# A decode kernel of four attention layers: the last four K tiles of each layer moved ahead of the last four V tiles, with four buffers for p

## The chip, the cores and the metric

The kernel runs on one core of a Trainium2 chip. The metric is the device time in microseconds (us), the median of several runs. Intervals are 95% intervals.

PE is the matmul engine, DVE the vector engine, ACT the scalar engine, SP the engine whose queue issues the large transfers (SPq in the profiles), DMA the 16 transfer engines. PEld is PE loading its weights, POOL the general-purpose engine, which does next to nothing here. The granted clock is the share of full speed at which PE was allowed to run. L541 in a profile is line 541 of that run's kernel. K28 is the K tile of a layer's head 28 in order of work, softmax 31 the softmax of its last head.

## The reference

One token goes through four layers, A, B, A, B. Each is attention over a cache of 8192 positions with 32 heads of 192, plus a residual:

```python
q = (layernorm(x) @ wq).reshape(32, 192)
scores = einsum("hd,hkd->hk", q, k_cache) * 192 ** -0.5      # k_cache: 32 x 8192 x 192, bf16
o = einsum("hk,hkd->hd", softmax(scores), v_cache)
x = x + o.reshape(1, 32 * 192) @ wo                          # x: 640
```

Every head brings a K tile and a V tile of 3.1 MB each, used once per layer. A and B are read twice, by layers 0 and 2 and by layers 1 and 3.

## The kernel before

The program is built from two lists. `steps` is the order of the work: `m` multiplies a K tile by q on DVE while PE sums the products, `s` is the softmax of one head, `v` the product with V on PE, `wc` and `wo` the turning and projecting of finished heads. `plan` is the order of the transfers. Tiles go into eight slots; a transfer is issued when the slot's previous tile is worked off.

```python
NSLOT = 8
KEPT = {0: {("k", 0), ("v", 0)}, 1: {("v", 28), ("v", 29), ("v", 30), ("v", 31)}}
...
            for p in range(H):
                if p > 0 and p % HEADS_W == 0:                 # p = 10, 20, 30
                    b = p // HEADS_W - 1
                    steps.append(("wc", l, b))
                    if p <= H - HEADS_W:
                        plan.append(("wo", l, b))
                        steps.append(("wo", l, b))
                if first_load("k", l, p) == ("k", l, p):
                    plan.append(("k", l, p))
                ...
                elif p < H - 2:
                    part = [("m", l, p), ("s", l, p), ("v", l, p)]
                elif p == H - 2:
                    part = [("m", l, p)]
                else:
                    part = [("s", l, p - 1), ("m", l, p), ("v", l, p - 1), ("s", l, p), ("v", l, p)]
                steps += part
                plan += [n for n in part if n[0] == "v" and first_load(*n) == n]
            ...
            plan.append(("wo", l, 2))
            steps.append(("wo", l, 2))
```

The program of every engine is written in the order of `steps`, so a V product that stands behind softmax 31 there does not start before PE's part of that softmax in the timelines below. The four V tiles of `KEPT[1]` stay in their slots from layer 1 to layer 3, so layer 2 has only four slots that turn over.

How one head's softmax and V product stand on the engines (cut):

```python
            def softmax(h):
                ev_s = DV.op(... tensor_reduce(s_sb[par][:], S[:] ...), ev_S[h], ...)      # waits for PE's sums
                ev_m = DV.op(... tensor_reduce(m_bf[par][:], s_sb[par][:], AX.X, ALU.max), ev_s, ...)
                e = PE.op(... matmul(QM[...], lhsT=m_bf ...), ev_m, ...)
                ev_n = DV.op(... tensor_reduce(negm[par][:], QM[...], AX.X, ALU.max, negate=True), e, ...)
                ev_p[h] = AC.op(... activation(p_sb[par][:], s_sb[par][:], ACT.Exp ...), ev_n, ...)
                e = PE.op(... matmul(TB[...], ... rhs=l_col ...), ev_p[h], ...)
                ev_rl[h] = ... DV.op(... reciprocal(rl[par][:], TB[...]), e, ...)          # the last step of a softmax

            def values(h):
                PE.wait(need(nv_), ev_p[h], last["O"][par])
                for m in range(J // 2):
                    e = PE.op(... matmul(OB[par][...], lhsT=p_sb[par][:, j:j + 2], rhs=t[...]) ...)
                ...                                        # ACT copies OB to o_sb, scaled; PE gathers o_sb later
```

## Time and profile before

| | before |
|---|---|
| median, us | 2004.94 of three runs, 2004.62 once a fourth was added |
| span of the profiled run | 2000.9 us |
| read from memory | 848.36 MB |
| rate where it is steady | 428 to 431 GB/s |

The page's slices (40 equal parts of the span; DMA is the busy share of the transfer engines in tenths, GB/s what they moved):

```profile
DMA  9999999999999999999999999999999999999997
GB/s 410 430 430 431 429 429 430 431 431 428 426 431 431 428 430 431 430 430 430 429 380 431 429 428 431 431 428 429 431 428 421 429 430 430 430 428 430 430 430 307
...
HBM read 848.36 MB, written 0.00 MB: 424 GB/s over the span
```

The rate is flat, so the kernel is bound by its transfers. The Trainium skill, "DMA: Bandwidth & Descriptors", Specifications, gives 435 GB/s as the ceiling of the fabric, and the 430 here agree with it. 848.36 MB at 430 GB/s are 1973 us; only the remaining 28 us of the span can be gained by reordering. The slices that fall well short are the first, the one of 380 in the middle and the last.

The windows around the middle one, the passage from layer 1 to layer 2. Columns: the stretch in us, its length, busy time (instructions) of PE, PEld, DVE, ACT and POOL, granted clock of PE, share of DMA, GB/s:

```profile
core 0: us, PE busy (x) PEld busy (x) DVE busy (x) ACT busy (x) POOL busy (x), PEclk, DMA share, GB/s
1004.00:1012.00 8.00, 7.03 (x54) 0.76 (x33) 4.58 (x6) 1.08 (x4) 0.00 (x0) 0.88 0.92 391
1012.00:1020.00 8.00, 6.23 (x149) 5.66 (x150) 0.17 (x1) 1.35 (x5) 0.00 (x0) 0.97 0.76 316
1020.00:1028.00 8.00, 5.82 (x96) 4.28 (x93) 3.58 (x12) 0.73 (x2) 0.54 (x1) 0.50 0.85 332
```

Here the rate drops to 316 GB/s: layer 2's wq comes in parts, and slots for them come free only as layer 1 ends. The end of layer 2, same columns:

```profile
1495.00:1500.00 5.00, 1.88 (x7) 0.50 (x4) 3.67 (x5) 0.44 (x2) 0.00 (x0) 0.75 1.00 428
1500.00:1505.00 5.00, 5.00 (x15) 0.00 (x0) 3.65 (x3) 0.00 (x0) 0.00 (x0) 0.57 0.99 422
1505.00:1510.00 5.00, 3.74 (x44) 1.05 (x35) 1.33 (x4) 1.15 (x4) 0.00 (x0) 1.00 0.90 367
```

One mild dip, to 367. And the end of the program, from the timeline (start, duration, engine, line, operation, tiles; in brackets what ended an idle time):

```profile
1984.53 1.47 PE L541 MATMUL O<-pool,p_sb 128*2 128x384 bf16 x32
...
1987.67 0.17 DVE L530 RECIPROCAL small<-TB 128x1 f32<-128x1 f32 x1 [1.18 <-PE TB L526]
...
1988.68 2.48 PE L541 MATMUL O<-pool,p_sb 128*2 128x384 bf16 x32
...
1991.21 0.94 ACT L556 ACTIVATE o_sb<-O,small 128x192 f32<-128x192 f32 x2 [2.25 <-PE O L541]
...
1992.21 1.44 PE L580 MATMUL TB<-small,o_sb 128*64 128x1 f32 x12 [1.04 <-ACT o_sb L556]
...
1993.58 2.56 PE L462 MATMUL YB<-oT,pool 128*128 128x1 bf16 x60
...
1997.38 0.16 DVE L628 TENSOR_TENSOR x_bf<-small,YB 128x5 bf16<-128x5 f32 x1 [9.54 <-PE YB L462]
```

Read it from L530 on, the end of softmax 31. Of the V work only V31 (32 matmuls, L541, at 1988.68) follows; V30 (at 1984.53) was already done inside the softmax. Then come the copy (L556), the gather (L580) and the projection (L462), and the result is there at 1997.4, 9.5 us after softmax 31.

### The profile page before, as it was taken

To read this page: it belongs to the slowest core of one execution; us is meant where nothing else is said; L and a number is where in the kernel's file an instruction comes from. 1 tells how busy PE (TensorE), PEld (TensorE's weight loads), DVE (VectorE), ACT (ScalarE), POOL (GpSimd) and SP (SyncE) were. 2 spreads that over 40 slices of the span, in tenths; PEclk is the share of its full clock that TensorE was granted. 3 is DMA by queue.
4 is the path that set the end of the run, shared out by engine and by line. 5 is a ranking of instruction groups with operands and counts; after the bars stand their busy time and mean duration, and the time that the engine had idled before them with its cause. 6 is when DMAs were issued, how large, how long until landed. Compare 5 with 4: busy or idle time off the path is not lost.

```text
span 2000.9 us, 20649 instructions
## 1 busy us (share of the span) xinstructions
PE 1404.3 (70%) x10555; PEld 323.1 (16%) x7611; DVE 1049.4 (52%) x1074; ACT 219.8 (11%) x665; POOL 4.5 (0%) x22
## 2 busy tenths in 40 slices
PE   4767767667666767766777667776767777767667
PEld 1111111111311111111131111121112212111112
DVE  3554544656255455455545545545554556554554
ACT  0111111111011111111101111111110111111111
POOL 0000000000000000000000000000000000000000
PEclk9887787888688788878977888888887888887887
DMA  9999999999999999999999999999999999999997
GB/s 410 430 430 431 429 429 430 431 431 428 426 431 431 428 430 431 430 430 430 429 380 431 429 428 431 431 428 429 431 428 421 429 430 430 430 428 430 430 430 307
DMA packets 40296, 849.69 MB, mean 425 GB/s; under 512 B 4688, under 2 KB 4688, under 8 KB 5136
## 3 DMA queue, kind: packets, MB, share of 16 engines
q1 hardware_dynamic: 40064, 848.38, 99.2%
q8 instruction: 71, 1.16, 0.2%
q14 instruction: 17, 0.14, 0.0%
q10 hardware_dynamic: 144, 0.00, 0.0%
HBM read 848.36 MB, written 0.00 MB: 424 GB/s over the span
## 4 chain that ended last, share of the span: by engine, by line
DMA 67%; PE 20%; DVE 11%; issue 1%; ACT 1%; SPq 0%; another core or an unknown queue 0%; DVEq 0%
DMA pool<-in_A_k_cache_dram 33%; DMA pool<-in_B_k_cache_dram 31%; PE S L58 13%; DVE pool L492 9%; PE O L541 2%; DMA pool<-in_B_wq_dram 1%; DMA x_bf<-in_A_x_dram 1%; DMA pool<-in_B_wo_dram 1%; PE S L505 1%; PE TB L564 1%; PE QT L424 1%; DVE s_sb L512 1%; PE YB L462 1%; ACT p_sb L522 0%; PE TB L526 0%
## 5 line engine op out<-in xcount | busy, mean ns | idle before, releaser
L492 DVE TENSOR_TENSOR pool<-pool,q_sb 128x3072 bf16<-128x3072 bf16 x512 | 865.6, 1753 | 423.4 <-DMA pool<-in_A_k_cache_dram 220.5
L58 PE MATMUL S<-pool,ident 128*128 128x512 bf16 x2944 | 805.5, 428 | 34.7 <-DVE pool L492 34.5
L541 PE MATMUL O<-pool,p_sb 128*2 128x384 bf16 x4096 | 346.7, 417 | 0.0
L512 DVE TENSOR_REDUCE s_sb<-S 128x64 f32<-128x512 f32 x128 | 88.5, 692 | 270.3 <-PE S L58 270.3
L505 PE MATMUL S<-pool,ident 128*128 128x512 bf16 x128 | 61.2, 478 | 224.5 <-DVE pool L492 224.5
L541 PEld LDWEIGHTS O<-pool,p_sb 128*2 128x2 bf16 x4096 | 130.4, 87 | 162.0 <-issue 126.2
L564 PE MATMUL TB<-o_sb,small 128*1 128x192 f32 x480 | 122.9, 389 | 36.4 <-DVE small L530 28.0
L450 ACT ACTIVATE q_sb<-QM 128x192 bf16<-128x192 f32 x120 | 39.7, 331 | 967.1 <-PE QM L443 967.1
L443 PEld LDWEIGHTS QM<-ident,qT 128*128 128x128 bf16 x240 | 23.2, 98 | 743.6 <-issue 728.1
L526 PE MATMUL TB<-small,ones 128*128 128x1 f32 x256 | 49.3, 262 | 110.9 <-ACT p_sb L522 110.9
L516 PE MATMUL QM<-ident,m_bf 128*128 128x128 bf16 x128 | 27.8, 217 | 129.0 <-DVE m_bf L515 129.0
L556 ACT ACTIVATE o_sb<-O,small 128x384 f32<-128x384 f32 (+1 forms) x136 | 77.4, 581 | 268.0 <-PE O L541 268.0
L530 DVE RECIPROCAL small<-TB 128x1 f32<-128x1 f32 x128 | 21.5, 168 | 122.9 <-PE TB L526 122.9
L522 ACT ACTIVATE p_sb<-s_sb,small 128x64 bf16<-128x64 f32 x128 | 44.4, 347 | 227.7 <-DVE small L519 227.7
L519 DVE TENSOR_REDUCE small<-QM 128x1 f32<-128x128 f32 x128 | 37.3, 291 | 52.6 <-PE QM L516 52.6
L570 ACT ACTIVATE orow<-TB 1x192 bf16<-1x192 f32 x120 | 38.4, 320 | 203.3 <-PE TB L564 203.3
L526 PEld LDWEIGHTS TB<-small,ones 128*128 128x128 f32 x256 | 38.5, 189 | 129.8 <-ACT p_sb L522 129.8
L505 PEld LDWEIGHTS S<-pool,ident 128*128 128x128 bf16 x128 | 12.7, 99 | 283.7 <-DVE pool L492 282.7
L564 PEld LDWEIGHTS TB<-o_sb,small 128*1 128x1 f32 x480 | 33.4, 89 | 77.8 <-DVE small L530 37.2
L516 PEld LDWEIGHTS QM<-ident,m_bf 128*128 128x128 bf16 x128 | 12.2, 96 | 199.4 <-ACT q_sb L450 133.9
L462 PE MATMUL YB<-oT,pool 128*128 128x1 bf16 x900 | 38.0, 178 | 2.5 <-ACT oT L476 2.2
L462 PEld LDWEIGHTS YB<-oT,pool 128*128 128x128 bf16 x900 | 37.0, 131 | 3.3 <-ACT oT L476 2.9
(50 smaller groups left out, 223.4 us busy)
## 6 DMA issues: line engine op xcount, KB each, us to landing
pool<-in_B_k_cache_dram SPq DMA_DIRECT2D x64, 3072.0 KB, 35.5
pool<-in_A_k_cache_dram SPq DMA_DIRECT2D x63, 3072.0 KB, 27.7
pool<-in_A_v_cache_dram SPq DMA_DIRECT2D x63, 3072.0 KB, 33.3
pool<-in_B_v_cache_dram SPq DMA_DIRECT2D x60, 3072.0 KB, 37.5
pool<-in_A_wo_dram SPq DMA_DIRECT2D x6, 2400.0 KB, 26.6
pool<-in_B_wo_dram SPq DMA_DIRECT2D x5, 2400.0 KB, 33.9
pool<-in_A_wq_dram SPq DMA_DIRECT2D x1, 7680.0 KB, 20.9
pool<-in_B_wq_dram SPq DMA_DIRECT2D x1, 7680.0 KB, 24.7
```

The costliest lines, as they stand in the source:

```text
L58: return t.add_instruction(mybir.InstMatmult(name=t.bass.get_next_instruction_name(), engine=mybir.EngineType.PE, ins=[t.lower_ap(rhs), t. ...
L450: lambda a: a.activation(q_sb[i][:], QM[:, 0:DH], ACT.Copy), e, last["q"][i], bank=use["QM"])
L462: e = PE.op(lambda t, i=i, c=c, f=y_first[0], fin=end and i == k - 1: t.matmul(YB[:, c:c + 1], lhsT=t3[:, i, c:D:DC], rhs=o[:, i:i + 1], s ...
L492: e = DV.op(lambda v, d0=d0: v.tensor_tensor(k3[:, :, d0:d0 + QD], kin[:, :, d0:d0 + QD], q_sb[qi][:, d0:d0 + QD].unsqueeze(1).broadcast_t ...
L505: t.matmul(S[:, :], lhsT=ident[:], rhs=k3[:, :, d0:d0 + R], start=True, stop=fin) if d0 == 0 else
L512: ev_s = DV.op(lambda v: v.tensor_reduce(s_sb[par][:], S[:].rearrange("p (j r) -> p j r", r=R), AX.X, ALU.add), ev_S[h], last["s"][par], b ...
L516: e = PE.op(lambda t: t.matmul(QM[:, C_MX:C_MX + P], lhsT=m_bf[par][:, 0:1].broadcast_to([P, P]), rhs=ident[:], start=True, stop=True), ev ...
L522: ev_p[h] = AC.op(lambda a: a.activation(p_sb[par][:], s_sb[par][:], ACT.Exp, bias=negm[par][:, 0:1], accum_out=l_col[par][:]), ev_n, ev_s ...
L526: e = PE.op(lambda t: t.matmul(TB[:, C_L + par:C_L + par + 1], lhsT=ones[:, 0:1].broadcast_to([P, P]), rhs=l_col[par][:], start=True, stop ...
L541: e = PE.op(lambda e, g=g, j=j, f=m < G, fin=fin: e.matmul(OB[par][32 * g:32 * g + 2, 0:2 * DH], lhsT=p_sb[par][:, j:j + 2], rhs=t[:, j * ...
L556: ev_os[h] = AC.op(lambda a, o=o, i=i: a.activation(o, i, ACT.Copy, scale=rl[par][:, 0:1]), e, ev_rl[h], last["osb"], bank=use[f"O{par}"])
L564: e = PE.op(lambda t, i=i: t.matmul(TB[0:1, C_O:C_O + DH], lhsT=pick[:, i:i + 1], rhs=o_sb[:, i * DH:(i + 1) * DH], start=(i == 0), stop=( ...
```

## The change

The intent: by the time the last K tile lands, its multiply, sums and softmax still take over 10 us. If the last K tiles come first, that work passes under the transfers of the V tiles. So each layer's transfers end with K28 to K31, then V28 to V31, then wo. Since four heads now wait between their softmax and their V product, p and the reciprocals get four buffers in place of two. The core of the diff (the indexing of the four buffers by `pi` and the rewritten head of the loop are cut):

```diff
+AHEAD = 4
-        p_sb = [sb(f"p_sb{i}", [P, J], BF16) for i in range(2)]
+        p_sb = [sb(f"p_sb{i}", [P, J], BF16) for i in range(AHEAD)]
-        rl = [col(1) for i in range(2)]
+        rl = [col(1) for i in range(AHEAD)]
...
-                elif p < H - 2:
-                    part = [("m", l, p), ("s", l, p), ("v", l, p)]
-                elif p == H - 2:
-                    part = [("m", l, p)]
                 else:
-                    part = [("s", l, p - 1), ("m", l, p), ("v", l, p - 1), ("s", l, p), ("v", l, p)]
+                    part = [("m", l, p), ("s", l, p)]
+                    if p < H - AHEAD:
+                        part.append(("v", l, p))
+                    elif p == H - 1:
+                        part += [("v", l, i) for i in range(H - AHEAD, H)]
+                        part.insert(-O_LAST, ("wc", l, 2))
                 steps += part
```

This edit moves the transfers (all K, then all V), and the work (all four V products after softmax 31).

## The prediction

> **What bounds the kernel now.** Transfers. The page's slices show 428 to 431 GB/s nearly everywhere; the Trainium skill ("DMA: Bandwidth & Descriptors", Specifications) gives 435 GB/s as the fabric's ceiling, and the trace agrees. 848.4 MB at 430 GB/s is 1973 us of the 2000.9 us span, so all stalls are worth 28 us. The windows put them at the start (a few us), between layers 1 and 2 (1008 to 1040 us, mostly 218 to 435 GB/s: about 6 us), layers 2 and 3 (1 us), layers 0 and 1 (none), and at the end (the stream thins out at 1984 to 1991 us, the last instruction comes 9 us later).
>
> **What the change does.** Bytes, multiplies and matmuls stay; the order at each layer's end moves. Call the landing of K28 t0; a 3.1 MB tile takes 7.3 us. Before: K28 V28 K29 V29 K30 K31 V30 V31 wo; after: all K, then all V. By bytes V31 lands at t0+51, wo at t0+57, in both.
>
> From the timeline: one K head takes 6.8 us of DVE multiply, 1.4 to 3.3 us until PE's sums end, 2.7 us softmax, serial in DVE's order: 11.0 us at full clock, 12 to 13 at half clock. In the old order K31's softmax ends at t0+52 to t0+55. In the new one four K land every 7.3 us and are worked off every 11 to 12: softmax 31 ends at about t0+46 (44 to 50), 8 us earlier.
>
> But PE's program puts all four V after softmax 31. Before, only a tail of 9.3 to 10.3 us followed it (gather 30, V31, copy, gather, projections). Now V28 2.2, copy 0.6, gather 0.8, V29 and the same, row copy and columns 1.5, V30 2.2, copy 1.0 come ahead of that tail: about 21.5 us in all, 23 if the clock falls. The layer's result comes at t0+67 to t0+69 instead of t0+61 (layer 1) or t0+65 (others). The gain in K is given back in V.
>
> **Critical path.**
> - Layers 0 to 1: wq and three tiles are queued; no change.
> - Layers 1 to 2: few slots turn over (four hold the kept V). The first wq part is queued 6 us earlier (gains about 1 us), but its second part waits for wo's projection, 5 to 6 us later, and K1 of layer 2 for the first multiply. Estimate +3.5 us.
> - Layer 2's end has four slots: V28 to V31 wait for K28 to K31's sums, V31 is issued at about t0+43 with the queue's end at t0+44. A DMA costs about 2 us fixed (same page, Anatomy; the output's write took 2.9 us here). Estimate +2.
> - End: the last landing is at t0+59, the result at t0+67 to 69: compute decides, +2 to +3 us.
>
> **Predicted time:** 2012 us, 80% between 2001 and 2022. Faster by over 2%: 0.005; within 2%: 0.975; slower: 0.02.
>
> **What would show it.** Softmax 31 earlier against K28's landing by about 8 us; about 20 us from it to the layer's result; a dip in GB/s near the end of layer 2, one as large as before or larger between layers 1 and 2, none between 0 and 1; 430 elsewhere.
>
> **What would make it wrong.** A higher granted clock in the K phase (11.0 us a head) and V at 1.5 us each would bring the layer's end 3 us earlier than I say: a tie. A low clock would stretch each K head to 13 us and stall layer 2's transfers more.

## The result, and the profile after

| | before | after |
|---|---|---|
| median, us | 2004.62 (4 runs, 2004.06 to 2006.3) | 2008.06 (4 runs, 2006.73 to 2010.38) |
| ratio of after to before | | 1.0017, interval 1.0000 to 1.0034 |
| profiled span, us | 2000.9 | 2005.2 |

A ratio is the mean time of one kernel's runs over that of the other's of the same rounds, so not quite the ratio of the medians. Executions over 1.5% slower than the fastest of the same kernel are left out of the means. The difference, 3.4 us, is on the slower side, with an interval that just reaches no difference. A second measurement below gives 1.0019. The slices after:

```profile
DMA  9999999999999999999989999999999999999997
GB/s 412 430 431 426 431 430 430 430 431 429 421 431 430 430 430 430 428 431 430 429 363 431 430 429 430 430 430 428 430 401 430 429 427 433 429 428 430 431 429 311
```

The dip in the middle (363) is there as before, and a new one (401) has come at the end of layer 2. The passage from layer 1 to 2:

```profile
1004.00:1012.00 8.00, 4.93 (x75) 2.26 (x75) 1.04 (x4) 2.04 (x6) 0.00 (x0) 1.00 1.00 427
1012.00:1020.00 8.00, 5.63 (x129) 4.39 (x130) 0.00 (x0) 2.45 (x7) 0.00 (x0) 1.00 0.74 311
1020.00:1028.00 8.00, 6.95 (x126) 5.91 (x127) 1.24 (x10) 0.34 (x2) 0.54 (x1) 0.59 0.53 189
```

The dip begins later, since the first part of wq is issued at 1005 us in place of 1011, and goes deeper, to 189. (That is no mark of the new order: in one of the runs below, old in layer 1, the last of these windows fell to 114 GB/s.) The end of layer 2:

```profile
1495.00:1500.00 5.00, 4.77 (x20) 0.00 (x0) 3.16 (x3) 0.00 (x0) 0.00 (x0) 0.91 0.64 275
1500.00:1505.00 5.00, 2.83 (x35) 1.24 (x35) 1.18 (x4) 0.90 (x3) 0.00 (x0) 0.77 0.91 319
1505.00:1510.00 5.00, 3.72 (x46) 1.66 (x47) 0.00 (x0) 1.34 (x4) 0.00 (x0) 0.89 0.98 417
```

275 and 319 GB/s in the two windows around 1500 us, where the lowest of the old order was 367. (The layer began 2.4 us later here, so equal windows are not quite equal places.) The reason stands in the timeline: the issue of V31 begins as DVE begins to read K31's finished sums.

```profile
1499.80 0.33 SPq L319 DMA_DIRECT2D pool<-in_A_v_cache_dram  x1
1499.81 0.69 DVE L513 TENSOR_REDUCE s_sb<-S 128x64 f32<-128x512 f32 x1 [1.84 <-PE S L58]
```

The end of the program:

```profile
1983.19 2.00 PE L543 MATMUL O<-pool,p_sb 128*2 128x384 bf16 x32
1983.29 0.17 DVE L531 RECIPROCAL small<-TB 128x1 f32<-128x1 f32 x1 [0.95 <-PE TB L527]
...
1986.78 1.93 PE L543 MATMUL O<-pool,p_sb 128*2 128x384 bf16 x26
...
1990.63 1.06 PE L473 MATMUL TB<-one_b,orow 1*128 1x1 bf16 x15 [0.41 <-ACT orow L572]
...
1991.63 1.47 PE L543 MATMUL O<-pool,p_sb 128*2 128x384 bf16 x32
...
1994.93 1.47 PE L543 MATMUL O<-pool,p_sb 128*2 128x384 bf16 x32
...
1998.24 2.56 PE L462 MATMUL YB<-oT,pool 128*128 128x1 bf16 x60
...
2002.04 0.16 DVE L630 TENSOR_TENSOR x_bf<-small,YB 128x5 bf16<-128x5 f32 x1 [18.58 <-PE YB L462]
```

Softmax 31 now ends at 1983.5 (L531), but all four V products come with it or later: L543 at 1983.19 (V28), at 1986.78 (the last part of V29), at 1991.63 (V30) and at 1994.93 (V31), with copies, gathers and the columns (L473) between. The result comes 18.6 us after softmax 31 in place of 9.5.

To see where the time comes from, I cut each profiled run at the starts of the multiplies, which the timeline gives. "K28" is the start of K28's multiply, which begins when the tile has landed. The numbers of the first three rows are differences of two such starts, in us; the others end with the softmax's last instruction (L530, L531) or with the start of the one that gives the layer's result:

| stretch | before | after |
|---|---|---|
| layer 0 to 1: K28 of layer 0 to K26 of layer 1 | 478.8 | 478.2 |
| layer 1 to 2: K28 of layer 1 to K1 of layer 2 | 86.3 | 88.6 |
| layer 2 to 3: K28 of layer 2 to K26 of layer 3 | 448.9 | 450.8 |
| end: K28 of layer 3 to the result | 64.9 | 65.3 |
| K28 to the end of softmax 31, layers 0 to 3 | 54.0, 52.2, 55.7, 55.3 | 46.1, 46.1, 45.8, 46.8 |
| end of softmax 31 to the layer's result | 10.2, 9.1, 10.3, 9.5 | 19.3, 18.1, 19.3, 18.6 |

The last two rows are the change in short: K's work is 6 to 10 us earlier, and the V work after it is 9 us longer. My theory at this point: the order of the work gives back what the order of the transfers gains, and two passages lose because few slots turn over there. Rivals: the order of the transfers costs by itself, the same in each layer; or the loss sits at the end of the program alone.

### The profile page after: what moved, and what is told of

Same layout as the page of the kernel before. It is cut to its first block, busy times and chain, and to the rows that moved or that the text cites. A ratio compares the mean times of both kernels' runs of the same rounds, so it can differ in the third digit from the quotient of the medians.

```text
span 2005.2 us, 20645 instructions
## 1 busy us (share of the span) xinstructions
PE 1396.5 (70%) x10555; PEld 320.9 (16%) x7611; DVE 1049.1 (52%) x1074; ACT 220.7 (11%) x665; POOL 4.5 (0%) x22
## 4 chain that ended last, share of the span: by engine, by line
DMA 60%; PE 23%; DVE 13%; ACT 1%; issue 1%; another core or an unknown queue 1%; DVEq 0%
DMA pool<-in_A_k_cache_dram 30%; DMA pool<-in_B_k_cache_dram 29%; PE S L58 15%; DVE pool L492 11%; PE O L543 2%; DVE s_sb L513 1%; PE S L505 1%; DMA x_bf<-in_A_x_dram 1%; PE TB L566 1%; ACT p_sb L523 1%; PE YB L462 1%; PE TB L527 1%; PE QT L424 1%; ACT o_sb L558 1%
## 5 line engine op out<-in xcount | busy, mean ns | idle before, releaser
L543 PE MATMUL O<-pool,p_sb 128*2 128x384 bf16 x4096 | 342.7, 416 | 0.0
L513 DVE TENSOR_REDUCE s_sb<-S 128x64 f32<-128x512 f32 x128 | 88.6, 692 | 258.7 <-PE S L58 258.7
L543 PEld LDWEIGHTS O<-pool,p_sb 128*2 128x2 bf16 x4096 | 128.4, 87 | 130.1 <-issue 94.9
L531 DVE RECIPROCAL small<-TB 128x1 f32<-128x1 f32 x128 | 21.6, 169 | 122.2 <-PE TB L527 122.2
## 6 DMA issues: line engine op xcount, KB each, us to landing
pool<-in_B_k_cache_dram SPq DMA_DIRECT2D x64, 3072.0 KB, 35.5
```

What stands on the lines that cost most here:

```text
L513: ev_s = DV.op(lambda v: v.tensor_reduce(s_sb[par][:], S[:].rearrange("p (j r) -> p j r", r=R), AX.X, ALU.add), ev_S[h], last["s"][par], b ...
L543: e = PE.op(lambda e, g=g, j=j, f=m < G, fin=fin: e.matmul(OB[par][32 * g:32 * g + 2, 0:2 * DH], lhsT=p_sb[pi][:, j:j + 2], rhs=t[:, j * D ...
```

## The experiments

All of these gave correct results. Kernels are compared only within the same rounds. Where the text says "old", "new" and "early", it means the form of a layer's end, set for each layer by a list:

```diff
+TAIL = ["old" | "new" | "early"] * 4
...
+                elif tail == "old":
+                    part = ([M, S, V(p)] if p < H - 2 else [M] if p == H - 2 else [S1, M, V(p - 1), S, V(p)])
...
+                elif p < H - 1:
+                    part = [M, S]                                               # new and early
+                elif tail == "new":
+                    part = [M, S, V(H - 4), V(H - 3), C, V(H - 2), V(H - 1)]
+                else:                                                           # early
+                    part = [V(H - 4), M, V(H - 3), S, C, V(H - 2), V(H - 1)]
```

M, S, V and C are the steps `m`, `s`, `v` and `wc`. With "new" everywhere the instructions of every engine come in the same order as in the kernel after, with "old" everywhere as in the kernel before. Four buffers are used in all.

### The new order in one layer alone

```diff
+TAIL = ['old', 'new', 'old', 'old']     # and 'new' in layer 2 alone, in layer 3 alone
```

Layer 1:

> New order in layer 1 alone, the old one in layers 0, 2 and 3. Theory (few free slots after layer 1: the second wq part of layer 2 waits for wo's projection, which comes later because V28 and V29 are worked off after softmax 31): +2.5 us over before (1.5 to 3.5), all of it gained between 1012 and 1030 us. Rival 1 (the order costs the same in each layer): +0.9 us. Rival 2 (the whole loss is at the end of the program, where V work follows softmax 31): 0.

Layer 2:

> New order in layer 2 alone. Theory (four slots: V31 can be issued only when K31's sums are done): +1.8 us (1 to 3), with a dip of the transfer rate below 330 GB/s in the 10 us around the issue of V31, which before has not. Rival 1: +0.9 us. Rival 2: 0.

Layer 3:

> New order in layer 3 alone. Theory (K31's softmax about 9 us earlier, the V work after it about 8 to 9 us longer): +0.5 us (-0.5 to +1.5). My prediction on record had +2 to +3 us here. Rival 1: +0.9. Rival 2: +3.5 us or more.

Measured against before (2005.24 us, 9 runs):

| new in | median, us | ratio and interval | its stretch in the profile, us | before |
|---|---|---|---|---|
| layer 1 | 2006.77 | 1.0010, 0.9997 to 1.0024 | layer 1 to 2: 89.7 | 86.3 |
| layer 2 | 2006.68 | 1.0013, 1.0000 to 1.0026 | layer 2 to 3: 452.7 | 448.9 |
| layer 3 | 2008.03 | 1.0011, 0.9998 to 1.0024 | end: 65.5 | 64.9 |

The times alone cannot part the theories: 0.1% each, with intervals as wide. (The three also add up to twice the whole change's 0.17%, which those intervals allow.) The profiles can, since each holds three old passages beside the new one. The stretch from layer 2 to 3 is 448.9 and 448.8 us in the two runs that are old there, and 452.7 in the run that is new. That profile is of the slowest of the run's five executions, 2010.42 us, so its size is at the upper end. In it V31 was issued at 1504.19, and the windows show what it cost:

```profile
1504.19 0.33 SPq L328 DMA_DIRECT2D pool<-in_A_v_cache_dram  x1
```

```profile
1500.00:1505.00 5.00, 4.16 (x16) 0.00 (x0) 1.79 (x3) 0.00 (x0) 0.00 (x0) 0.84 0.14 59
```

59 GB/s for 5 us: the transfers had nothing else to do. The tile landed 11.3 us after its issue, where tiles in a full queue land every 7.3 us. Layer 2's loss is shown: with four slots the stretch took 448.5 to 449.1 us in all six profiles that are old there, and 450.8 to 452.7 in the three that are new.

Layer 1 went against me. The stretch from layer 1 to 2 took 91.1 and 89.5 us in the two runs that are *old* there, as long as the 89.7 of the new one or longer. Of what I had called a loss of 2.3 us between the two kernels' profiles, nothing is left: before's profile was one quick passage of an order that varies (that profiled execution, 2003.06 us, was quicker than all of the timed ones). The 2.5 us expected between 1012 and 1030 us are not there. The rival of a cost at the end alone fell too.

### One more draw of the old passage

```diff
+TAIL = ['old', 'old', 'old', 'old']
```

> Only the four buffers for p and for the reciprocals, the order of before. The same program as before in every instruction, so 0 us, within 0.1 per cent. Its profile is one more draw of the passage from layer 1 to layer 2 in the old order: from K28 of layer 1 to K1 of layer 2 before took 86.3 us, and the runs with the old order in layer 1 alone took 91.2 and 89.5; if that passage varies by itself, as I now think, this one lies anywhere between 86 and 92.

2003.92 us against 2005.75, ratio 0.9996 (0.9981 to 1.0012): no effect of the buffers alone is seen, to within 0.2%. The passage took 88.3 us. PE's clock in it varies along with its length. The windows from 26 to 51 us after K28 of layer 1 began, for the kernel before, for this run and for the run with layer 2 alone new, all three old in layer 1:

```profile
986.50:1011.50 25.00, 18.69 (x139) 3.36 (x87) 16.00 (x15) 2.43 (x8) 0.00 (x0) 0.93 0.98 417
```

```profile
986.30:1011.30 25.00, 19.72 (x130) 3.60 (x88) 15.69 (x15) 1.84 (x6) 0.00 (x0) 0.80 0.99 424
```

```profile
986.10:1011.10 25.00, 19.95 (x101) 3.19 (x60) 14.80 (x12) 1.85 (x6) 0.00 (x0) 0.73 0.99 424
```

Granted clock 0.93, 0.80, 0.73; softmax 31 ended 52.2, 53.5 and 55.7 us after K28; passage 86.3, 88.3 and 91.1 us. Two further draws of the old order (clock 0.80 in both) took 88.9 and 89.5. The Trainium skill, "TensorE: Matmul & The Clock Gate", Part 1, says that an idle PE falls back to half clock, that activity releases it, and that the window in which this is judged runs freely, so that the same kernel meets it at another phase each time. The traces agree as far as they go: in every run here the granted clock is either full or half and changes only on a grid of 3.413 us, and the start of K28 of layer 1 lies 2.35, 0.42, 1.20, 2.85 and 2.89 us into a step of that grid in the five old passages of 86.3, 88.3, 91.1, 89.5 and 88.9 us. Near-equal places (the last two) went with near-equal passages. That the place on the grid sets the length is not shown: no run changed it alone.

### The place of V28 and V29 in PE's program

```diff
+TAIL = ['early', 'early', 'early', 'early']
```

> The order of transfers of after in all layers, but PE's program takes V28 ahead of K31's sums and V29 between them and K31's softmax, instead of both after it; V30 and V31 stay behind. Theory (what is lost is lost through the place of V28 and V29 in PE's program): from softmax 31 to the layer's result about 12 us instead of 18 to 19, the end of the program 4 us earlier, between layers 1 and 2 no loss against before, layer 2 still 1 to 2 us slower from its slots: in all -4 us against before (-7 to -1). Rival (the order of transfers itself is at fault, not the order of the work): +3.4 us as after.

The fourth corner, the transfers of before with the work of after:

```diff
-                plan += [n for n in part if n[0] == "v" and first_load(*n) == n]
+                vload = [n for n in part if n[0] == "v"] if p < H - AHEAD else (
+                    [("v", l, p)] if p < H - 2 else [("v", l, p - 1), ("v", l, p)] if p == H - 1 else [])
+                plan += [n for n in vload if first_load(*n) == n]
```

> The fourth corner: transfers in the order of before, but PE works off V28 and V29 after softmax 31 as in after, in all layers. Theory (the place of V28 and V29 in PE's program is what costs): about 6 us at the end of the program, 5 to 8 us between layers 1 and 2, about 8 us after layer 2 from its slots, none after layer 0: +20 us against before (12 to 28). Rival (the order of transfers costs, the place of the work does not): 0.

The four corners (each ratio against before of its own rounds; us from the ratio and before's median):

| | V28 and V29 before softmax 31 ends | after it |
|---|---|---|
| old transfers | before: 0 | e5: 1.0168 (1.0151 to 1.0186), +34 us |
| all K, then all V | e4: 0.9972 (0.9960 to 0.9985), -5.6 us | after: 1.0017, +3.4 us |

In either order of transfers, holding V28 and V29 back costs: 9 us in the new order, 34 in the old one, where they also hold slots the longer (about 11 of the 34 come from where the planner then put a wq, told below). In either order of work, all K first gains: 6 and 30 us. (In the old transfers V30 stands before softmax 31's end too, and is held back with V28 and V29 in e5.) So the rival that blames the order of the transfers is out: that half of the change gains, and the other half costs more than that. The end of the early form (same columns as before; L552 is the V product, L540 the end of softmax 31):

```profile
1966.72 1.47 PE L552 MATMUL O<-pool,p_sb 128*2 128x384 bf16 x32
...
1975.59 1.62 PE L552 MATMUL O<-pool,p_sb 128*2 128x384 bf16 x26
...
1978.71 0.17 DVE L540 RECIPROCAL small<-TB 128x1 f32<-128x1 f32 x1 [1.01 <-PE TB L536]
...
1984.66 2.06 PE L552 MATMUL O<-pool,p_sb 128*2 128x384 bf16 x32
...
1993.01 0.16 DVE L640 TENSOR_TENSOR x_bf<-small,YB 128x5 bf16<-128x5 f32 x1 [14.13 <-PE YB L471]
```

V28 at 1966.7 lies in a wait that PE had anyway, before the sums of K31, and the main part of V29, at 1975.6, between those sums and the end of softmax 31; after it only V30 and V31 follow. V31's transfer landed at 1984.6 and its product began at 1984.66: in this run the transfers, not the work, set the end. The result came 59.5 us after K28.

Two points of the expectation failed. From softmax 31 to the result it took 13.9 to 16.8 us in the four layers, not about 12. And layer 2 was to lose 1 to 2 us still, and its stretch took 448.9 us, as long as in the old order. The early V28 gives its slot back early too, and the planner gave that slot to V31: it was issued 35.5 us after K28 began, in place of 43.1.

The fourth corner missed its range: +34 us in place of 12 to 28. The end (71.1 in place of 64.9 us) and the stretch from layer 2 to 3 (457.8) came about as written, the passage from layer 1 to 2 (97.3) 8.5 us over the old order's mean where 5 to 8 were written, but layer 0 to 1 took 489.6 where I expected 478.6. SP's queue and the windows show it:

```profile
490.16 0.33 SPq L341 DMA_DIRECT2D pool<-in_A_wo_dram  x1
517.05 1.56 SPq L314 DMA_DIRECT2D pool<-in_A_wo_dram  x2
```

```profile
510.00:520.00 10.00, 7.47 (x160) 5.67 (x161) 0.00 (x0) 2.73 (x8) 0.00 (x0) 1.00 0.08 19
```

After wo (L341) nothing was issued for 27 us, until V31, the last product of the layer, had been worked off (L314). I had overlooked that layer 1's whole wq needs three neighbouring slots; here the planner took those of V30, V28 and V31. 19 GB/s for 10 us is the price. In the kernel after, wq follows K31, V28 and V29; V29's slot came free at 504.3 us, before the queue was empty, and layer 0 costs nothing.

### A fifth slot for layer 2

```diff
-KEPT = {0: {("k", 0), ("v", 0)}, 1: {("v", 28), ("v", 29), ("v", 30), ("v", 31)}}
+KEPT = {0: {("k", 0), ("v", 0)}, 1: {("v", 29), ("v", 30), ("v", 31)}}
```

With the old order, then with the new one:

> One V tile less is kept from layer 1 to layer 3, so layer 2 has five slots in place of four; the old order. One tile more to load: +7.3 us against before, less what the fifth slot saves between layers 1 and 2 (0 to 3 us): +4 to +7.5 us.

> The same with the new order. Theory (in layer 2 the fifth slot lets V31 be issued earlier than K31's sums): the stretch from K28 of layer 2 to K26 of layer 3, less the tile more, as long as with the old order, within 0.7 us, in place of 1.8 to 3.7 us longer; in time +0.5 us (-1 to +2) over e7. Rival (layer 2's loss is from the V work after softmax 31 and not from the slots): still 2 to 4 us longer.

Times 2010.7 us (ratio 1.0026) and 2008.65 us (1.0018): the new order is 1.6 us quicker by the two ratios, just below my range of -1 to +2. The stretch from layer 2 to 3 took 456.2 us old and 456.1 us new: with a fifth slot the loss is gone, though the V work stands after softmax 31 as before. In the run with the new order V31 was issued 30.8 us after K28, in place of 43.1 to 45.5, and the windows show:

```profile
1495.00:1500.00 5.00, 3.10 (x15) 0.39 (x3) 2.01 (x4) 0.44 (x2) 0.00 (x0) 1.00 1.01 433
1500.00:1505.00 5.00, 4.32 (x67) 1.83 (x68) 0.17 (x1) 0.90 (x2) 0.00 (x0) 0.66 0.97 413
```

No dip where four slots gave 275 and 319. So, by one profile of each, layer 2's loss comes from the lack of slots and not from the late V work as such. It takes both: with four slots the early form lost nothing there either. It does not pay as a whole, since a V tile more must be loaded. The fifth slot also shortened the passage from layer 1 to 2, to 83.7 and 84.0 us.

### Which layers the early form needs, and the new order once more

```diff
+TAIL = ['old', 'old', 'old', 'early']
+TAIL = ['old', 'early', 'old', 'early']
+TAIL = ['new', 'new', 'new', 'new']
```

> The early form (all K first, but V28 and V29 in PE's program ahead of softmax 31) in layer 3 alone, layers 0 to 2 as before. Theory: only the end of the program changes, from 64.8 us after K28's multiply starts to 59.5: -5.3 us against before (-4 to -6.5).

> The early form in layers 1 and 3, layers 0 and 2 as before. Theory: layers 0 and 2 add nothing either way, so as the early form in all layers, -6 to -8 us against before; and against the early form in layer 3 alone 0 to -3 us, since layer 1's result comes at about 61 us after K28 in place of 61 to 66.

> The kernel after the change once more, the same instructions, on the same chip as the two others: +3 us against before (1 to 5). Its profile is one more draw of the passage from layer 1 to layer 2 (K28 to K1 of the next layer) in the new order. If that passage is the result's time plus about 25 us, and the result comes at 64 to 65 us, it takes 88.5 to 90 us, inside the 86.3 to 91.1 of four passages in the old order. Rival: the new order does cost 2 to 3 us there, then above 91. After layer 2 again 1.8 to 3.8 us more than the old order's 448.9.

| | median, us (before 2005.79) | ratio and interval | layer 1 to 2 | layer 2 to 3 | end |
|---|---|---|---|---|---|
| early in layer 3 | 2001.37 | 0.9977, 0.9965 to 0.9990 | 88.9 | 448.8 | 61.5 |
| early in 1 and 3 | 1999.08 | 0.9964, 0.9951 to 0.9976 | 85.6 | 448.5 | 61.3 |
| new everywhere | 2009.58 | 1.0019, 1.0005 to 1.0032 | 89.6 | 451.2 | 63.4 |

All three times came inside their ranges. The early form in layers 1 and 3 beats both kernels, by 7 us and by 10 to 11; the form in all layers (1999.11, ratio 0.9972 on another chip) cannot be told from it. The new order's end took 63.4 us this time, less than the old one's 64.6 to 64.9. The early form's end took 61.5 and 61.3 us in place of 59.5: here V31's product began 54.4 and 53.0 us after K28, though V31 had landed at 51.2 and 51.1, so in these two runs PE, and not the transfers, came last.

With all draws together the passage from layer 1 to 2 is the time of layer 1's result plus about 25 us. The result came 61.3 to 65.9 us after K28 in the old order (mean 63.8), 64.1 to 65.9 in the new one (mean 64.9), 72.8 in the fourth corner, 61.2 twice in the early form; from it to the end of the passage it took 24.8 to 25.3 us in the old order and 23.8 to 24.8 in the new one. The new order's result thus came about 1 us later on average, and what followed was under 1 us shorter. The means are 88.8 us for five old passages, 89.3 for three new ones and 85.8 for two early ones.

## Why the prediction was right or wrong

Total: 2012 us predicted, 2008.06 measured, in the range. The direction and the mechanism held; the terms did not all. The range, 2001 to 2022, would have held a gain as well, and the forecast of about +7 us is twice the measured +3.4, so the hit of the total by itself says little: two of its three terms came out at about nothing.

- **Bound by transfers, 28 us to gain at most.** Held. The best version found took 7 of them.
- **Softmax 31 at t0+46.** Held: 45.8 to 46.8.
- **"About 21.5 us in all, 23 if the clock falls" from softmax 31 to the result.** Mis-sized: 18.1 to 19.3. I took 2.2 us for each V product; three of the four at the end took 1.5 to 2.0 us, and V29's began inside V28's gather.
- **Layers 0 to 1, no change.** Held, 478.2 against 478.8.
- **Layers 1 to 2, "Estimate +3.5 us".** Wrong. The result of layer 1 "at t0+61" was one draw at a granted clock of 0.93; the old order's passages took 86.3 to 91.1 us, mean 88.8, and the new order's 88.6 to 89.7, mean 89.3. The step that failed is taking one profile's passage for the kernel's: the old order's result came at 63.8 us on average, not at 61. The mis-sized tail did the rest: the new order's came at 64.1 to 65.9 us, not at 67 to 69. What is left is +0.5 us, less than the scatter.
- **Layer 2's end, "V31 is issued at about t0+43 with the queue's end at t0+44. Estimate +2".** Held. V31 was issued 43.1, 43.8 and 45.5 us after K28 in three runs, and the stretch took 1.9, 2.3 and 3.8 us more than 448.9: the later the issue, the larger the loss. V31 landed 11.4, 10.9 and 11.3 us after its issue, against 7.3 us a tile in a full queue. The Trainium skill, "DMA: Bandwidth & Descriptors", Anatomy, says that transfer engines don't wait on semaphores, the issuing sequencer does; the trace agrees, V31's issue stands at 1499.80 us, where K31's sums end.
- **End, "+2 to +3 us".** Mis-sized, for the same reason as the tail: the new order took 63.4 to 65.5 us, the old 64.6 to 64.9, so about nothing.

Mean effects of the stretches: 0.5 between layers 1 and 2, 2.7 after layer 2 (three draws), 0 at the end, 3.2 in all. The two measurements of the whole were +3.4 and +3.8 us (ratios 1.0017 and 1.0019). Where the expected gain went is thus named: K31's softmax does end 6 to 10 us earlier, but PE's program put two V products, two copies, two gathers and the columns behind it, and at the end of layer 2 the freed order met a lack of slots. What stays open is why the clock in the passage differs from run to run; the skill's account fits the traces but was not tested.

## What to carry to other kernels

Reordering transfers and reordering work are two changes, even where one list makes both: put each finished piece of work where its engine waits anyway, and hold back only what has not landed. Here that turned +3.4 us into -5.6, and into -7 where it was done in layers 1 and 3 alone. And when a change is worth 0.2%, one profile of each kernel isn't enough to size a passage: look at the same passage in every run where the code there is the same, and take the scatter from those.

## What the Trainium skill lacked or had wrong

- "DMA: Bandwidth & Descriptors", Specifications, lists about 358 GB/s as the limit of memory for one core, and its section on where 436 GB/s comes from says that this side binds for loads from memory. Neither place gives the condition that the same page has beside its measurements, that both cores of a pair stream; for one alone it measured 425 GB/s. Here one core loaded at 428 to 431 GB/s for nearly all of 2000 us, so with one core at work the fabric's figure is the one to use.
- "TensorE: Matmul & The Clock Gate", Part 1, calls the ramp's cost under 1% of a typical span and advises against fitting it. No run here measures that cost for the whole kernel. But a passage of 86 to 91 us varied by 4.8 us (0.24% of the total) between runs with the same instructions there, with granted clocks of 0.93 to 0.73, and that is more than the effect of the whole change. No page was found that says to take more than one profile for such a comparison.
- "DMA: Bandwidth & Descriptors" fits the time of one transfer for those that GpSimd issues, and for those that SP issues gives only a latency to the first byte. Here a tile of 3.1 MB, issued by SP into a queue that had run empty, landed 11.3 us after its issue, where tiles in a full queue land every 7.3 us.
